# Gated mix of two state-space convolutions: a Tanh gate, a dummy sine, one batch's one-input steps on VectorE, and a new order of the first fifth

## The chip, the cores and the metric

One core of a Trainium2 chip. TensorE (PE in the profile) multiplies matrices into PSUM, VectorE (DVE) and GpSimd (POOL) work element by element, ScalarE (ACT) evaluates functions from a table that it holds and copies, and the SP queue issues most DMAs. The metric is the device time of one execution in microseconds.

## The reference

A gate mixes two S4D convolutions of the same input x of 2048 steps by 512 channels, with 128 modes to a channel:

```python
g = _sigmoid((x * gate_w).sum(-1, keepdims=True))
a = _A_ref(x, A_log_A_real, A_A_imag, A_C_real, A_C_imag, A_log_dt, A_D_skip)
b = _B_ref(x, B_log_A_real, B_A_imag, B_C_real, B_C_imag, B_log_dt, B_D_skip)
return g * a + (1 - g) * b
```

Each of the two computes, with L = 2048:

```python
dt = jnp.exp(log_dt)
A = -jnp.exp(log_A_real) + 1j * A_imag
C = (C_real + 1j * C_imag) * dt[:, None]
P = jnp.exp((A * dt[:, None])[:, :, None] * pos[None, None, :])
K = 2.0 * jnp.einsum("dn,dnl->dl", C, P).real
y = jnp.fft.irfft(Uf * Kf[None, :, :], L2)[:, :, :L]
return y + u * D_skip[None, None, :]
```

## The kernel before, in words

**What is computed where.** The 2 x 512 channels form 8 chunks of 128, worked on in 64 units of 16 channels. A unit makes its convolution kernels from two small grids. TensorE makes the phases (`phase`, L509), exact up to whole turns, by fp16 matmuls of the angles (`rot`, and a constant, `ones`) with a table of times (`cph`). ScalarE takes the magnitude (`magnitude`, L518) and a sine of it as the cosine (`cosine`, L525), and the sine (`sine`, L522). GpSimd multiplies decays into grids (`grid0`, `grid1`, L530) from the bases `bas`, VectorE multiplies sines and cosines into the grids (L551 to L573), TensorE sums over the modes (`modes`, L575). Then come a fast Fourier transform in three matmul steps (`first`, `s2`, then products with the transform of the input on VectorE, `inverse`) and the last step (`final`, `last`), whose matrix `eg` has the gate in it.

**The gate.** `gate` (L778) sums x times gate weights over the channels into all partitions by matmuls; `gate_sig` (L786) takes the sigmoid on ScalarE, with a scale per partition (`sgn`, +1 for kernel a, -1 for b); `gate_e` (L789) multiplies it into a quarter of `eg` on VectorE. There are four quarters, j = 0 to 3; their input is loaded by 16 DMAs `load_ut` (256 KB each).

**The preparation.** Chunks are prepared in five batches: 0; 1 and 2; 3 and 4; 5 and 6; 7. `decay_rate` (L333) takes an Exp of the decay rates on ScalarE. `prep_ops` (L338) makes, in about 35 steps, the angles per step and of the amplitudes: some steps on VectorE or ScalarE by their source or function (`magnitudes`, `larger`, `signs` at L376, `angle` at L384, an Arctan and two Sin), and the others on an engine `E`, VectorE for batch 0 and GpSimd for the later ones. Among those, the one-input steps are `theta` (L380), all that `ts` makes (L392: scaling, rounding to whole turns) and `diag` (L416, a scaled identity). `bounce` spills the angles to DRAM, `turns` (L489) reads them back transposed into `rot`, `turned` (L421) transposes decays and amplitudes by matmuls, `dec` (L429) multiplies them by times, and `make_bases` (L495) takes four Exp a chunk from them into `bas`; `amplitudes` (L500) finishes them on GpSimd.

**Tables on ScalarE.** Before an instruction whose function the table at hand doesn't hold, the compiler puts a table load into ScalarE's queue.

**The order.** The program makes a list of 2494 operations, each of a few instructions, with names such as `al` (`decay_rate`), `ex` (`make_bases`), `gs` (`gate_sig`), `gu` (`load_ut`), `wu` (groups of warm-up matmuls, L286, whose results nobody reads). `ORDER` (L33) is a permutation of that list. It sets the order of every engine's queue, each working through its own in order. `SLOTS` (L191) gives the PSUM bank, of eight, for each PSUM tile in order of allocation.

## Time and profile before

| | |
|---|---|
| runs, us | 501.21, 501.22, 504.62 (median 501.22) |
| profiled execution, us | 500.83 |
| its span, us | 498.9 |
| granted TensorE clock, mean | 0.983 |

Busy time over the span, and instructions:

| engine | busy us | share | instructions |
|---|---|---|---|
| TensorE, matmul | 443.1 | 89% | 12448 |
| TensorE, weight load | 357.4 | 72% | 12448 |
| VectorE | 392.9 | 79% | 864 |
| ScalarE | 405.2 | 81% | 816 |
| GpSimd | 332.9 | 67% | 316 |

The chain that ended last lies 61% on TensorE over the whole span, 12% on ScalarE, 8% on VectorE and 7% on GpSimd. How to read the rows that follow: a row of the timeline or of the chain has start, duration, engine, source line, operation, output and inputs, and in brackets the idle time in front and what ended it. A row of a group has the count, then total busy us and mean ns, then idle time in front. A row by stage has the stretch, its length, and each engine's busy time with its number of instructions. L numbers are lines of the kernel before.

### The profile page before, as it was taken

What the parts mean: (1) busy time and instruction counts of PE and PEld (TensorE: products, weight loads), DVE (VectorE), ACT (ScalarE), POOL (GpSimd) and SP (SyncE); (2) the same over time, 40 slices, a digit from 0 to 9 for tenths busy, and PEclk for the clock granted to TensorE, in tenths of its full rate; (3) what the DMA queues carried; (4) which work ended last, traced back from release to release, by engine and by line L of the source; (5) the groups of instructions that cost most, each with busy time, mean ns of one, the idle gap of its engine ahead of it and who ended that gap; (6) DMA issues with size and microseconds to landing.
All of it is one profiled execution on the core that took longest, in us unless ns stands there. A gap on an engine that the chain in (4) does not pass through costs nothing.

```text
span 498.9 us, 27908 instructions
## 1 busy us (share of the span) xinstructions
PE 443.1 (89%) x12448; PEld 357.4 (72%) x12448; DVE 392.9 (79%) x864; ACT 405.2 (81%) x816; POOL 332.9 (67%) x316
## 2 busy tenths in 40 slices
PE   5967997988999887997999898978998899989988
PEld 5855556876778675875888686767777779767984
DVE  6394898899999975888889795787999898976402
ACT  5697999989899987788998997777999797964323
POOL 1497998899997977686667866385775754862000
PEclk9998999999999999998999998999999999999999
DMA  4669705316550704246430744134443733174201
GB/s 143 226 235 287 186 11 126 69 25 123 136 94 12 150 27 98 69 77 157 79 61 11 150 105 74 57 78 96 113 77 60 157 65 67 36 169 74 59 25 60
DMA packets 32279, 48.92 MB, mean 98 GB/s; under 512 B 10144, under 2 KB 17440, under 8 KB 32160
## 3 DMA queue, kind: packets, MB, share of 16 engines
q1 hardware_dynamic: 27360, 31.41, 22.2%
q0 software_dynamic: 4800, 15.73, 19.0%
q8 instruction: 97, 1.59, 1.3%
q14 instruction: 22, 0.18, 0.1%
HBM read 17.25 MB, written 5.77 MB: 46 GB/s over the span
## 4 chain that ended last, share of the span: by engine, by line
PE 61%; ACT 12%; DVE 8%; issue 8%; POOL 7%; DMA 5%; SPq 0%; DVEq 0%; ACTq 0%; POOLq 0%
PE ps L640 15%; PE psi L694 11%; PE pk L581 9%; PE p0s L514 7%; PE ps L603 5%; DMA xall<-xall 5%; PE pf L718 4%; POOL f L530 3%; PE psu L603 3%; ACT bas L498 2%; ACT xall L610 2%; PE pw L289 2%; PE pw L293 2%; PE psg L782 1%; DVE xall L651 1%
## 5 line engine op out<-in xcount | busy, mean ns | idle before, releaser
L530 POOL TENSOR_TENSOR f<-bas 128x1024 f32<-128x1024 f32 (+1 forms) x128 | 207.7, 1689 | 78.6 <-PE pk L581 45.4
L640 PE MATMUL ps<-xall,gk 128*64 128x64 f32 (+1 forms) x1728 | 111.3, 251 | 5.7 <-DVE f L553 1.7
L640 PEld LDWEIGHTS ps<-xall,gk 128*64 128x64 f32 (+1 forms) x1728 | 101.4, 153 | 19.1 <-issue 2.7
L651 DVE TENSOR_TENSOR xall<-ps,v 128x256 f32<-128x256 f32 x256 | 94.5, 415 | 15.5 <-PE ps L640 13.4
L581 PE MATMUL pk<-f,f 128*32 128x64 f32 x4096 | 74.3, 223 | 15.5 <-issue 7.2
L581 PEld LDWEIGHTS pk<-f,f 128*32 128x32 f32 x4096 | 62.9, 111 | 27.6 <-issue 17.2
L694 PE MATMUL psi<-mi,xall 128*128 128x128 f32 x512 | 71.8, 287 | 4.4 <-issue 2.7
L681 POOL DMA_DIRECT2D xall<-xall x60 | 60.1, 1152 | 17.4 <-DVE f L557 8.1
L694 PEld LDWEIGHTS psi<-mi,xall 128*128 128x128 f32 x512 | 63.5, 196 | 10.2 <-issue 5.0
L557 DVE TENSOR_TENSOR f<-f,p0c 128x512 f32<-128x512 f32 x64 | 43.6, 682 | 14.4 <-ACT p0c L526 13.8
L514 PE MATMUL p1s<-cph,ones 64*128 64x512 f16 x128 | 49.3, 386 | 3.2 <-DVE ks L591 2.1
L553 DVE TENSOR_TENSOR f<-f,p0c 128x512 f32<-128x512 f32 x64 | 43.6, 681 | 8.6 <-ACT p0c L526 7.9
L603 PEld LDWEIGHTS ps<-w,ks 64*64 64x64 f32 x2048 | 35.4, 140 | 20.7 <-issue 7.7
L514 PE MATMUL p0s<-cph,ones 64*128 64x512 f16 x128 | 49.4, 386 | 0.5 <-ACT xall L610 0.4
L514 PE MATMUL p1s<-cph,rot 64*128 64x512 f16 x128 | 49.0, 382 | 0.8 <-issue 0.8
L569 DVE TENSOR_TENSOR f<-f,p1c 128x512 f32<-128x512 f32 x64 | 43.6, 682 | 7.3 <-ACT p1c L526 5.6
L610 ACT COPY xall<-ps 128x512 f32<-128x512 f32 x64 | 36.9, 612 | 15.0 <-PE ps L603 15.0
L603 PE MATMUL ps<-w,ks 64*64 64x64 f32 x2048 | 40.3, 227 | 9.6 <-issue 6.3
L514 PE MATMUL p0s<-cph,rot 64*128 64x512 f16 x128 | 48.9, 382 | 0.0
L701 ACT COPY z<-psi 128x512 f32<-128x512 f32 x64 | 37.9, 609 | 12.7 <-PE psi L694 12.7
L573 DVE TENSOR_TENSOR f<-f,p1s 128x512 f32<-128x512 f32 x64 | 43.6, 681 | 5.2 <-ACT p1s L523 4.1
L565 DVE SCALAR_TENSOR_TENSOR f<-f,p0s 128x512 f32<-128x512 f32 x64 | 43.4, 680 | 3.2 <-ACT p0s L523 3.0
(128 smaller groups left out, 824.1 us busy)
## 6 DMA issues: line engine op xcount, KB each, us to landing
xall<-xall POOLq DMA_DIRECT2D x60, 256.0 KB, 5.2
v<-v SPq DMA_DIRECT2D x64, 128.0 KB, 3.3
uraw<-in_us SPq DMA_DIRECT2D x16, 256.0 KB, 3.8
z<-in_ut SPq DMA_DIRECT2D x16, 256.0 KB, 6.4
out_dram<-ot SPq DMA_DIRECT2D x28, 128.0 KB, 2.2
par<-in_par SPq DMA_DIRECT2D x8, 256.0 KB, 4.4
gk<-in_gk SPq DMA_DIRECT2D x4, 512.0 KB, 6.1
eg<-in_eg SPq DMA_DIRECT2D x4, 512.0 KB, 5.6
```

The source lines that it names most:

```text
L514: PE.matmul(ps, w[h : h + 64], cph[h : h + 64, j], start=j == 0, stop=j == 3, tile_position=(h, 0))
L530: G.tensor_tensor(o.rearrange("p k (a b) -> p k a b", b=8), x[:, :, hi : hi + n].unsqueeze(3).to_broadcast([128, 16, n, 8]), x[:, :, lo : ...
L553: V.tensor_tensor(f0[:, 0, :, 0:32], f0[:, 1, :, 0:32], half(u, p0c[u], True), OP.mult)
L557: V.tensor_tensor(f0[:, 0, :, 32:64], f0[:, 1, :, 32:64], half(u, p0c[u], False), OP.mult)
L569: V.tensor_tensor(f[:, 0], f[:, 1], p1c[u], OP.mult)
L581: PE.matmul(pk[32 * kd : 32 * kd + 32, i, :], f1[:, p, 4 * i + kd, :], f0[:, p, 4 * i + kd, :], start=p == 1, stop=p == 0, tile_position=( ...
L603: PE.matmul(ps[h][64 * ri : 64 * ri + 64, n, :], x[r], w1[r, ri, r], start=True, stop=True, tile_position=(64 * h, 64 * ri),)
L610: S.copy(o, pxs[key][h])
L640: PE.matmul(ps[h : h + w, j, 0:n], gk[:, k, h : h + w], xall[:, x0:x1, 2 * k : 2 * k + 2], start=True, stop=True, tile_position=(0, h),)
L651: V.tensor_tensor(k.rearrange("p x (k t) -> p k x t", t=2), p2s[b, g][:, :, 0:64].rearrange("p k (x t) -> p k x t", t=2), vv.unsqueeze(3). ...
L681: G.dma_start(out=xk(b)[o, s], in_=t2[t, s], accum_op=OP.add)
L694: PE.matmul(ps[:, i, :], t[:, x : x + 2, :].rearrange("p x k -> p (x k)"), w, start=n == 0, stop=n == len(parts) - 1,)
```

## The change

Six things, in code:

- The gate's Sigmoid becomes a Tanh of half the argument (`sgn` is +0.5 and -0.5), and `gate_e` multiplies `eg` by 1 + tanh; the factor 1/2 of sigmoid(x) = (1 + tanh(x/2))/2 goes into the constant `eg`.
- A new operation `tw` takes a Sin of the one-column tile `warm`, which nobody reads. The clearing of `warm` becomes an operation of its own (`fw`).
- In `prep_ops` the one-input steps `theta`, `ts` and `diag` run on an engine `F`, VectorE for batches 0 and 1 and GpSimd for the later ones. The steps with two inputs stay on `E`.
- The list has 2496 operations, and the numbers in `ORDER` are shifted by the two new ones.
- The order is another one up to position 547 of the list (545 before), which is where chunk 2's `turns` stands, next to unit 10's and 11's operations. Behind it the sequence is the one from before.
- `SLOTS` is new. Behind the 115th PSUM tile the banks are those from before, renamed by one permutation.

```diff
@@ fixed @@
-        V.memset(warm, 0.0)
...
     op("fx", fixed)
+    op("fw", V.memset, warm, 0.0)
@@ prep_ops @@
         E = V if i == 0 else G
+
+        F = V if i < 2 else G
...
         def theta():
             for n, c in enumerate(cs):
-                E.tensor_scalar(get("t0")[:, n], pars[i][:, n, 0], dti[:, c : c + 1], None, op0=OP.mult)
+                F.tensor_scalar(get("t0")[:, n], pars[i][:, n, 0], dti[:, c : c + 1], None, op0=OP.mult)
...
         def ts(o, x, s0, s1, op0, op1=None):
             kw = dict(op1=op1) if op1 is not None else {}
-            return lambda: E.tensor_scalar(get(o), get(x), s0, s1, op0=op0, **kw)
+            return lambda: F.tensor_scalar(get(o), get(x), s0, s1, op0=op0, **kw)
...
         def diag():
             d["dg"] = prep.tile([128, 2, 128], F32, name="dg", tag="dg")
             for n, c in enumerate(cs):
-                E.tensor_scalar(d["dg"][:, n], ident, dt2[:, c : c + 1], None, op0=OP.mult)
+                F.tensor_scalar(d["dg"][:, n], ident, dt2[:, c : c + 1], None, op0=OP.mult)
@@ new, behind amplitudes @@
+    def table(f):
+        S.activation(warm, warm, f)
@@ gate_sig, gate_e @@
     def gate_sig(j):
-        S.activation(psg[j], psg[j], AF.Sigmoid, scale=sgn)
+        S.activation(psg[j], psg[j], AF.Tanh, scale=sgn)
...
         g = psg[j].rearrange("p (r m) -> p r m", m=M)
-        V.tensor_tensor(e, e, g.unsqueeze(1).to_broadcast([128, 2, 16, M]), OP.mult)
+        V.scalar_tensor_tensor(e, g.unsqueeze(1).to_broadcast([128, 2, 16, M]), 1.0, e, op0=OP.add, op1=OP.mult)
@@ batch @@
+        if i == 0:
+            op("tw", table, AF.Sin)
         op("al", decay_rate, i)
@@ _layout @@
-    eg = np.stack([np.cos(ph), -np.sin(ph)], 1) / 2048
+    eg = np.stack([np.cos(ph), -np.sin(ph)], 1) / 4096
...
-    small = np.concatenate([ldt, 1 - 2 * kern[:, None], gw, times], 1)
+    small = np.concatenate([ldt, 0.5 - kern[:, None], gw, times], 1)
```

What the new order moves, queue by queue (numbers in parentheses are units, chunks or quarters; a batch's name stands for its step):

- ScalarE, front. Before: magnitudes of batch 0, an input copy, angle, `al`, high parts, low parts, an input copy, the four `ex` of chunk 0, two input copies, magnitude and cosine of unit 0. Now: magnitudes, `al`, an input copy, angle, high parts, low parts, an input copy, the four `ex`, two input copies, `tw`, magnitude and cosine of unit 0.
- ScalarE, gates. Before: `al` of batch 2, the four `ex` of chunk 1, a copy, gates 0 and 1; later gates 3 and 2, parts of batch 1, a copy, the `ex` of chunk 2. Now: `al` of batch 2, a copy, one `ex` of chunk 1, gate 1, the magnitudes of batch 2, `ex`, gate 0, `ex`; later, behind unit 6's last sine, `ex` of chunk 1, gate 2, low parts of batch 1, `ex` of chunk 2, gate 3, a copy, and the other three `ex` of chunk 2.
- TensorE, front. Before four groups of warm-up matmuls stand ahead of batch 0's `turned` and two behind the second input transform; now three stand ahead of `turned`, one between it and the second input transform, two behind that.
- VectorE, front. The clearing of `ones` and `rot` goes behind `dec` of batch 0, the scaled identity of batch 0 ahead of the high parts. Batch 1's scaled identities stand behind that, ahead of unit 0's products; its other one-input steps stand between products of units 1 to 5.
- GpSimd. Batch 1's one-input steps are gone from between the grids of units 0 to 5. From unit 9's large grid to unit 11's small one, its list has batch 2's steps 10 and 16 of `prep_ops` (counted from 0), which stood ahead of that, and no longer its step 8.
- SP queue, front. Ahead of batch 0's `bounce` stand five `load_ut` where three stood; `cph` is issued between `bounce` and `turns` of chunk 0, where it stood ahead of both; `dl` goes behind `gk`. The 16 `load_ut` and four `load_e` are mixed anew up to about the first gates, and `turns` of chunk 2 goes behind the first two turns of `v` of the second block.

## The prediction

> **What bounds the kernel now.** I read the page first, then the busy time by stage, then the chain of waits over the stretch whose order changes, then ScalarE's timeline there.

> ```profile
> span 498.9 us, 27908 instructions
> ```
> ```profile
> core 0: us, PE busy (x) PEld busy (x) DVE busy (x) ACT busy (x) POOL busy (x), PEclk, DMA share, GB/s
> 24.00:42.00 18.00, 10.86 (x349) 8.40 (x348) 15.99 (x31) 16.18 (x34) 17.23 (x18) 1.00 0.76 255
> 42.00:62.00 20.00, 19.03 (x407) 11.89 (x407) 12.63 (x24) 18.50 (x35) 16.28 (x20) 0.91 0.80 222
> 62.00:86.00 24.00, 20.40 (x378) 12.87 (x368) 22.35 (x43) 23.85 (x41) 22.22 (x24) 0.98 0.24 61
> 86.00:106.00 20.00, 19.64 (x429) 17.04 (x430) 18.62 (x39) 18.40 (x39) 18.21 (x18) 0.94 0.32 62
> 106.00:126.00 20.00, 17.06 (x492) 13.02 (x490) 19.44 (x41) 18.17 (x38) 19.51 (x20) 1.00 0.50 102
> ```
> ```profile
> 7.65 8.41 PE pw L289 x64
> ...
> 17.89 3.06 ACT bas L498 x4
> ...
> 38.79 3.11 issue
> ...
> 81.16 1.28 ACT L526
> ...
> 89.54 1.95 POOL f L530
> ```

> The new order ends at about 106 us (unit 10's last sine product on VectorE); behind that every queue holds the same instructions in the same order, and the PSUM banks are only renamed. So the question is how much sooner the engines reach that point. From 106 to 126 us VectorE and GpSimd are busy 19.4 and 19.5 of 20 us, so a shift of all engines there should pass to the end whole, and a lead of GpSimd alone should not.

> In the stretch itself ScalarE is the tightest: 23.85 of 24 us in the third row, 76.9 of 82 in the first four. The chain says the same: it starts on the warm-up matmuls, goes through the four base exponentials, stalls once on the tensor engine (38.79, waiting for nothing that the trace shows), runs on ScalarE around both pairs of gates, table loads such as that at 81.16 among them, and only from 89.54 on lies on GpSimd for long. That GpSimd is busy 17.23 of 18 us early on is for the most part beside it.

> **The front.** The rows of ScalarE's timeline, with start, duration and line:

> ```profile
> 8.29 1.28 ACT L385 ACT_TABLE_LOAD   x1
> 9.59 0.31 ACT L385 ACTIVATE rc<-rc 128x128 f32<-128x128 f32 x1
> 9.92 1.28 ACT L386 ACT_TABLE_LOAD   x1
> ...
> 11.74 1.28 ACT L336 ACT_TABLE_LOAD   x1
> ...
> 14.47 0.52 ACT L409 ACTIVATE sp<-tb 128x384 f16<-128x384 f32 x1 [0.62 <-DVE tb L406]
> ...
> 23.07 0.58 ACT L520 ACTIVATE p0c<-p0s 128x512 f32<-128x512 f32 x1 [1.17 <-PE p0s L514]
> 23.67 1.28 ACT L526 ACT_TABLE_LOAD   x1
> 24.96 0.58 ACT L526 ACTIVATE p0c<-p0c 128x512 f32<-128x512 f32 x1
> ```

> The decay exponential (L336) moves ahead of the angle, to a place where ScalarE waits for the input transform, with or without a load of its own; the arctangent and the sine keep their two loads, since the dummy sine stands behind the exponentials of the bases and not ahead of the arctangent. The exp load thus leaves 11.74 and comes back ahead of the base exponentials. The turned matmuls stand behind three groups of warm-up matmuls and no longer four: 8.41/4 = 2.10 us sooner. On ScalarE the low parts (L409) end at about 14.5, a copy and the load follow, and the exponentials can start at about 16.3, 1.6 before their 17.89. The dummy sine then loads its table in the 1.17 us in which ScalarE waits for the first phase, so that the cosine follows the magnitude at once. The tensor engine still has six warm-up groups, both input transforms and the turned matmuls in front of the first phase, end to end, so that this starts at most 0.35 us sooner than now; the magnitude then starts at about 22.7 and the cosine at 23.3, where it starts at 24.96: **-1.65 us**. GpSimd's first grid gets its bases some 1.6 us sooner too, and the two scaled identities of batch 1 (L419) leave the space between its grids.

> What is moved past what: on the SP queue five gate inputs now go ahead of the first spill of the angles and not three; cph (512 KB, used by the first phase) goes behind that spill. It is issued near 15.2 instead of 9.05, about 6.4 us ahead of the phase. Nearest price:

> ```profile
> cph<-in_cph SPq DMA_DIRECT2D x1, 512.0 KB, 5.8
> ```

> So 0.6 us are left. If cph lands in its old 5.8 us I cost it at nothing; if traffic costs it 2 us more, the front's gain is gone and no more, since the phase is what it holds up.

> **The gates.** Sigmoid (L787) has its own load each time, between one for Exp and one for Sin (the load at 81.16 in the chain is the second pair's):

> ```profile
> 44.20 0.41 ACT L385 ACTIVATE rc<-rc 128x256 f32<-128x256 f32 x1
> ...
> 59.65 1.28 ACT L787 ACT_TABLE_LOAD   x1
> ...
> 72.56 1.28 ACT L787 ACT_TABLE_LOAD   x1
> ```

> In the new order both pairs of gates stand among the exponentials. If Tanh is served by the table that serves Exp, two loads go: 2 x 1.30 (a load and the gaps of 0.01 to 0.02 around it) = **-2.6 us**, both in a stretch where ScalarE is full. The bounds: no table shared, six loads more (a rival below); shared, two fewer. The nearest row is the sine table, under which batch 1's arctangent (L385 at 44.20) starts without a wait and without a load in front of it; tables here hold several functions, so I take sharing. A switch costs what the rows show, 1.28 plus 0.02. [...]

> The new product of the gate is a two-operation instruction instead of a plain one; a pair of such forms of equal size:

> ```profile
> L557 DVE TENSOR_TENSOR f<-f,p0c 128x512 f32<-128x512 f32 x64 | 43.6, 682 | 14.4 <-ACT p0c L526 13.8 <-POOL f L530 0.3
> L565 DVE SCALAR_TENSOR_TENSOR f<-f,p0s 128x512 f32<-128x512 f32 x64 | 43.4, 680 | 3.2 <-ACT p0s L523 3.0
> ```

> 682 against 680 ns: nothing. The halved constants are made on the host.

> **Batch 1's one-input steps.** On GpSimd, grouped over 25 to 62 us by line (L394, L382, L419; busy, count):

> ```profile
> 25.00:62.00 37.00, 7.76 (x8) 0.95 0.78 237
> 25.00:62.00 37.00, 1.18 (x2) 0.95 0.78 237
> 25.00:62.00 37.00, 1.20 (x2) 0.95 0.78 237
> ```
> ```profile
> L394 DVE TENSOR_SCALAR tb<-tb 128x128 f32<-128x128 f32 x4 | 0.9, 222 | 0.0
> ```
> ```profile
> L378 DVE TENSOR_SCALAR sg<-par x5: 286/596/1078, 4.9 to 224.8; 128x512 f32<-128x512 f32 x3, 128x256 f32<-128x256 f32 x2
> ```

> GpSimd loses 10.1 us. I give that no gain of its own: the chain lies on it only from 89.54, and from that grid to unit 11's small grid its new list has one step of batch 2 more than the old one (7.76/8 = 0.97 us at most), for which the 1.8 us that it idles in the fourth row are the cover. VectorE gains twelve instructions, two of them in front, where it waits for the phase. The ten others cost 0.29 us each (the 128x256 minimum), 2.9 us.

> But they may have to wait. The five instructions of L378 are the only one-input SBUF ones that VectorE runs beside grids. The one of 286 ns ran before the grids; the other of that size, at 224.79, took 1078 and ended just after GpSimd's small grid did, so it waited 0.79. By 64 ns more per 128 elements (222 to 286) the 128x512 ones should take about 414 and took 610 on average. That is 0.2 for three, 0.79 for one: 0.35 us on average. Bounds: 0 and a whole grid, 1.95 (the row at 89.54). I take 0.35, so ten cost 6.4 us. Behind each waits the unit's product and then the modes on the tensor engine. What hides them: VectorE idles 2.0 + 7.4 us in the first two rows, of which 1.5 lie ahead of its first product, behind the cosine that ends at 25.54. That leaves some 7.7, so 6.4 fit, barely; the ScalarE gain of the first pair of gates takes another 1.3 of it. VectorE is what is late next. Part of the cover is the stall at 38.79; if it is gone, the ten cost up to 2 us.

> **Sum:** 500.83 us for the profiled run (1.9 outside the span of 498.9) - 1.65 - 2.6 = 496.6. The median of the runs, 501.22, lies 0.4 above the profiled one: forecast **497.0 us**.

> **Rivals.**
> *More comes free.* With loads spread differently the stall at 38.79 goes and ScalarE's wait behind it with it. ScalarE idles 5.1 us in the first four rows; half of that gives 494.4, all of it 491.9. For: ScalarE is short of work there only in that one place. Against: VectorE has no room to follow. Chance 0.25.

> *VectorE becomes the bound.* Each of the ten waits out half a large grid, 0.98 us: 12.7 us, less 7.7 of idle time, is +5.0; the front's and the second pair's gains (-1.65 - 1.3) leave +2.0, so 503.3; with half the idle time unusable +5.9, 507.1. It decides from a mean wait of 0.78 us, or 0.39 if only half the idle time can be used. For: the 1078 ns. Against: three of four waited 0.2. [...] Chance 0.2.

> *Tanh is not in exp's table.* Then the change doesn't save loads: gates and exponentials alternate, six loads around each pair of gates for three now, 6 x 1.30 = +7.8, less 1.65: 507.4. [...] Chance 0.05.

> *The front is late*, cph or the spilled angles holding up the first phase: 498.6 and up to 501. Chance 0.1.

> **Numbers.** Forecast 0.4 (495 to 499). Within 1% of 501.22 (what a measurement of this kernel can tell from no change), 496.2 to 506.2, lie some two thirds of the forecast, the late front, a part of the first rival and most of the second: 0.43. Faster by more: a third of the forecast and most of the first rival, 0.41. Slower by more: the third rival and the second's upper part, with some room for a cost not seen, 0.16. The range runs from the first rival's end, 491.9, to past the second's middle: 491.5 to 504.

> **What would show it.** Right: two table loads fewer, none between base exponentials and gates; the first cosine at 23.3; the sine load behind the second pair of gates, now 81.16, near 77; unit 10's last product on VectorE some 4 us sooner; from there the same distance to the end. Wrong: VectorE's L394 of 128x256 at a mean over 1.0 us, and VectorE full from 42 to 62 us; a first phase that starts after 21.95; a lead at 106 us that shrinks later.

## The result, and the profile after

| | before | after |
|---|---|---|
| executions, us | 501.21, 501.22, 502.39, 504.62 | 505.52, 506.03, 509.24, 509.49 |
| median, us | 501.81 | 507.63 |
| ratio, 95% interval | | 1.0101 [1.0059, 1.0143] |
| profiled execution, us (clock) | 500.83 (0.983) | 506.03 (0.99) |

The kernel became 1% slower; 497.0 was forecast. Ten more executions of after, in a later run, gave 505.57 against 502.75 (1.0069 [1.0032, 1.0106]). Executions of one and the same kernel lie up to 16 us apart in these runs. So every ratio has its interval; it is taken over undisturbed executions alone, the medians over all, and the two can differ.

The head of after's page, and its busy time by stage in the stretches shown of before:

```profile
span 503.5 us, 27931 instructions
```
```profile
core 0: us, PE busy (x) PEld busy (x) DVE busy (x) ACT busy (x) POOL busy (x), PEclk, DMA share, GB/s
24.00:42.00 18.00, 12.12 (x416) 10.04 (x420) 16.51 (x32) 16.07 (x35) 9.27 (x9) 1.00 0.67 227
42.00:62.00 20.00, 18.70 (x394) 11.08 (x384) 18.95 (x35) 19.57 (x39) 14.86 (x15) 1.00 0.80 235
62.00:86.00 24.00, 21.52 (x442) 14.33 (x444) 23.45 (x47) 23.85 (x44) 23.61 (x26) 1.00 0.43 99
86.00:106.00 20.00, 17.58 (x349) 15.32 (x338) 16.57 (x36) 16.13 (x34) 19.07 (x20) 0.91 0.12 23
106.00:126.00 20.00, 16.22 (x488) 12.82 (x488) 19.93 (x36) 18.51 (x39) 19.33 (x18) 1.00 0.55 112
```

GpSimd's 17.23 us of the first stretch are 9.27, and VectorE's 12.63 of the second are 18.95: VectorE gained 6.8 us in the first two stretches, where 6.4 were forecast. ScalarE still idles 1.9 us in the first stretch, where it idled 1.8 (the two loads that went lay behind it). The order did what it says. ScalarE's timeline:

```profile
17.02 3.05 ACT L500 ACTIVATE bas<-dec 128x896 f32<-128x896 f32 x4
...
22.33 0.20 ACT L509 ACTIVATE warm<-warm 128x1 f32<-128x1 f32 x1
23.56 0.58 ACT L526 ACTIVATE p0c<-p0s 128x512 f32<-128x512 f32 x1 [1.03 <-PE p1s L520]
24.18 0.58 ACT L532 ACTIVATE p0c<-p0c 128x512 f32<-128x512 f32 x1
...
77.25 1.28 ACT L532 ACT_TABLE_LOAD   x1
```

The first cosine (L532) starts at 24.18, before at 24.96. The sine load behind the second gates is at 77.25, before at 81.16, and there is no load between base exponentials and gates: the gate at 71.34 (L793) follows an exponential at 70.42 (L500) without one, and after has 23 table loads in all for 25 in before. Tanh does sit in exp's table. At unit 12, behind the part that was reordered, this is the magnitude on ScalarE in after and in before:

```profile
111.45 0.62 ACT L526 ACTIVATE p0c<-p0s 128x512 f32<-128x512 f32 x1
```
```profile
113.68 0.62 ACT L520 ACTIVATE p0c<-p0s 128x512 f32<-128x512 f32 x1
```

So this pair of executions has a lead of 2.2 us there, in place of 4.2, and in the unchanged rest it turns into a loss of 4.6. One execution each shows little of a lead of that size: in the profiles below, the same start lies between 110.39 and 113.85 us in before's order (117.09 with 96 fewer) and between 110.05 and 113.85 in after's with Tanh.

**Where the rest lost it.** These are pieces of before's chain of waits past 120 us, the longest of those in which an engine waits for nothing that the profile names (start and duration in us):

```profile
175.27 2.45 issue
193.89 2.83 issue
233.85 1.18 issue
300.37 2.26 issue
342.84 1.51 issue
438.49 1.70 issue
491.45 1.38 issue
```

and of after:

```profile
125.67 2.88 issue
175.15 2.37 issue
193.35 3.24 issue
213.12 1.19 issue
234.64 1.21 issue
290.52 1.49 issue
302.80 2.28 issue
316.61 1.57 issue
343.72 2.31 issue
446.15 2.11 issue
464.42 1.13 issue
488.42 1.68 issue
```

Past 170 us these are seven pieces with 13.3 us in before and eleven with 20.6 in after, in the same work in the same order. Number all rows of the tensor engine in the trace (weight loads, matmuls, semaphore events) from 0, and divide the number by 256: the remainder (mod) is the same for all of these stalls in after past 170 us. Some of them:

```
after: number  mod 256  resumes at  idle  end of the last 16 KB instruction packet
        7105     193      177.52    2.37    176.00
        8129     193      196.58    3.23    195.13
        9153     193      214.31    1.19    212.89
       13249     193      292.01    1.49    290.44
       14017     193      305.08    2.28    303.66
```

All 17 stalls over 0.5 us in after that wait for no semaphore stand at position 193 of 256, and the engine goes on 1.20 to 1.56 us after a packet of this queue, a row of after's profile page, has landed:

```profile
q8 instruction: 97, 1.59, 1.3%
```

Two kinds can be told apart. In the first, the page is short. Half of after's packets start 0.9 to 1.7 us after the page in front of them has been entered (median 1.1); a packet takes about 1 us, and the engine can go on some 1.45 us later. By these medians, a page that is passed in under some 3.6 us should end in a stall (an estimate), and that hangs on which 256 instructions make up the page. In after, of the pages with no late packet, 12 of the 17 passed in less than that ended in a stall of over 0.1 us, and 4 of the 65 others. In the second, the packet is late; counted here as late is one that starts 2.4 us or more after that (the latest, 7.0). At 175 and 194 us in after it starts 4.2 to 4.5 us after, about when the engine stops or later. So it is (4.9 us) at 38.79 in before, the stall of 3.11 that the prediction could not name, which stands at position 193 too. Late packets make up 14.1 of after's 28.1 us of stalls at position 193, and 13.3 of before's 23.9. What makes a packet late isn't shown.

After has the same 12,448 matmuls, and 17 semaphore events more on the tensor engine than before (181 for 164), all of them in the reordered part. So the whole unchanged rest sits 17 places further on in its pages. That is the first theory (**pages**). It has two rivals. One is the renamed PSUM **banks**. The other is VectorE held up by GpSimd (**lock**), for which this row of after speaks, beside its like in before:

```profile
122.62 3.34 DVE L380 TENSOR_SCALAR sg<-par 128x512 f32<-128x512 f32 x1
```
```profile
124.69 0.50 DVE L378 TENSOR_SCALAR sg<-par 128x512 f32<-128x512 f32 x1
```

The sign step of batch 3, unchanged, took 2.8 us longer, the tensor engine stood still for 2.8 beside it, and the whole lead of 2 us was gone at unit 15.

### The profile page after: what moved, and what is told of

It reads as the page before. It is cut to its first block, busy times and chain, and to the rows that moved or that the text cites. A ratio compares the mean times of both kernels' runs of the same rounds, so it can differ in the third digit from the quotient of the medians.

```text
span 503.5 us, 27931 instructions
## 1 busy us (share of the span) xinstructions
PE 439.7 (87%) x12448; PEld 355.6 (71%) x12448; DVE 401.0 (80%) x876; ACT 404.0 (80%) x815; POOL 322.9 (64%) x304
## 3 DMA queue, kind: packets, MB, share of 16 engines
q0 software_dynamic: 4800, 15.73, 18.9%
## 4 chain that ended last, share of the span: by engine, by line
PE 52%; ACT 13%; issue 10%; POOL 9%; DVE 9%; DMA 6%; SPq 1%; DVEq 0%; ACTq 0%
PE ps L646 14%; PE psi L700 11%; PE pk L587 8%; PE p0s L520 6%; POOL f L536 5%; PE ps L609 4%; PE pf L724 4%; DMA v<-v 2%; ACT xall L616 2%; PE psu L609 2%; PE pw L292 2%; DVE xall L657 1%; DMA gk<-in_gk 1%; DVE f L579 1%; ACT p1c L526 1%
## 5 line engine op out<-in xcount | busy, mean ns | idle before, releaser
L563 DVE TENSOR_TENSOR f<-f,p0c 128x512 f32<-128x512 f32 x64 | 43.6, 681 | 12.8 <-ACT p0c L532 10.5
L559 DVE TENSOR_TENSOR f<-f,p0c 128x512 f32<-128x512 f32 x64 | 43.6, 682 | 10.1 <-ACT p0c L532 10.1
L520 PE MATMUL p0s<-cph,rot 64*128 64x512 f16 x128 | 48.2, 376 | 3.2 <-issue 3.2
L520 PE MATMUL p1s<-cph,ones 64*128 64x512 f16 x128 | 48.6, 380 | 2.1 <-DVE f L563 1.2
L609 PEld LDWEIGHTS ps<-w,ks 64*64 64x64 f32 x2048 | 34.9, 137 | 20.6 <-issue 8.0
L520 PE MATMUL p0s<-cph,ones 64*128 64x512 f16 x128 | 48.8, 381 | 0.5 <-DVE f L563 0.4
L520 PE MATMUL p1s<-cph,rot 64*128 64x512 f16 x128 | 48.1, 376 | 0.2 <-issue 0.2
L571 DVE SCALAR_TENSOR_TENSOR f<-f,p0s 128x512 f32<-128x512 f32 x64 | 43.4, 679 | 2.3 <-ACT p0s L529 2.0
## 6 DMA issues: line engine op xcount, KB each, us to landing
gk<-in_gk SPq DMA_DIRECT2D x4, 512.0 KB, 7.8
eg<-in_eg SPq DMA_DIRECT2D x4, 512.0 KB, 6.9
```

The costliest lines, as they stand in the source:

```text
L520: PE.matmul(ps, w[h : h + 64], cph[h : h + 64, j], start=j == 0, stop=j == 3, tile_position=(h, 0))
L559: V.tensor_tensor(f0[:, 0, :, 0:32], f0[:, 1, :, 0:32], half(u, p0c[u], True), OP.mult)
L563: V.tensor_tensor(f0[:, 0, :, 32:64], f0[:, 1, :, 32:64], half(u, p0c[u], False), OP.mult)
L609: PE.matmul(ps[h][64 * ri : 64 * ri + 64, n, :], x[r], w1[r, ri, r], start=True, stop=True, tile_position=(64 * h, 64 * ri),)
```

## The experiments

Each time stands against executions of before taken beside it. "Fewer" and "more" count tensor instructions in front of everything else, and the place is that count, with 17 added for after. The columns that the warm-up multiplies stay the same, and nobody reads its results.

**Moving the pages.** The forecast of the theory was worked out from the traces: take the start of each numbered instruction, leave the stalls at 193 out, cut the list into pages of 256, and sum what each page past 70 us lacks of 3.6 us; a shift moves the cuts. This sum is the forecast lack.

```diff
 def warm_up(n):
     pw = bank("pw")
-    for i in range(8):
-        PE.matmul(pw[:, 0:128], ident, ident, start=True, stop=True)
+    for w in WIDTHS.get(n, [128] * 8):
+        x = ident[:, 0:w] if w <= 128 else ident.unsqueeze(1).to_broadcast([128, w // 128, 128])
+        PE.matmul(pw[:, 0:w], ident, x, start=True, stop=True)
```

After, `WIDTHS = {2: [512, 256, 128, 128]}`:

> After, with the last warm-up group on the tensor engine cut to four matmul calls that cover the same 1024 columns (512, 256, 128, 128 instead of eight of 128): the same tensor time within 0.1 us, but 16 instructions fewer ahead of everything else, so that the rest of the tensor engine's list falls on nearly the same 256-instruction pages as in before. Nothing of the output hangs on it. Page theory (the lost time of the second half is the tensor engine waiting for its own instructions at position 193 of a page, and the change lost it by 17 more instructions in front): summed over the pages of after's trace, the shortfall against 3.6 us a page goes from 14.6 to 10.7 us, so the time falls by 2.5 to 4.5 us, to 503 to 505; VectorE's long sign step of batch 3 near 123 us may stay. Lock theory (VectorE held up by GpSimd is the whole loss): no change, 505.5 to 509.5. Bank theory (the renamed PSUM banks): no change.

Before, `{1: [128] * 4 + [64] * 8}`:

> Before, with its last warm-up group made of twelve matmul calls for the same 1024 columns (four of 128, eight of 64): 16 instructions more in front, nothing else touched, and nothing of the output hangs on it. Page theory: the shortfall against 3.6 us a page goes from 10.0 to 18.9 us, of which the stall at 38.79 (3.1 us) goes and the later ones grow, so 3 to 8 us slower than before, 505 to 510, with the new stalls all at position 193 of a page and new ones near 213 and 290 us as in after. Lock theory and bank theory: no change, 501 to 503, or 3 us faster by the stall at 38.79.

After as it is:

> After once more, unchanged, on the chip of the runs beside it, so that they have a base of their own. All theories: 1.0% over before, 503 to 510 by the granted clock. The sign step of batch 3 near 123 us: the lock theory, if the long step is a matter of the moment at which it is issued, gives either 0.5 us or more than 3 us; if it belongs to after's order, more than 3 us again.

After, `{2: [512, 512], 5: [512, 512]}`:

> After, with its last two warm-up groups made of two matmul calls of 512 columns each: 48 instructions fewer in front, the same columns. The page theory has a number for every shift: summed over the pages of six traces, the shortfall against 3.6 us a page is 14.6 us for after, 10 for 16 fewer, and has its least value, 4.6, at 48 fewer. A sixteenth-step of 4 us was worth 3.4 us between the two runs of the first call, so 10 us should be worth 6 to 8.5: 499 to 502 by the granted clock, 2 to 4 us faster than before. The stalls at position 193 past 170 us should sum to under 12 us, where after has 24 to 28. Lock and bank theories: as after.

Before, `{1: [512, 512], 2: [256, 256, 128, 128, 128, 128]}`:

> Before, with its last two warm-up groups made of two calls of 512 columns, and of two of 256 and four of 128: 32 instructions fewer, the same columns. Page theory: the shortfall past 70 us goes from 10.0 to 3.5 us, and the 3.1 us at 38.79 go, so 4 to 6 us faster than before, 496 to 500, with no more of after's parts in it. Lock and bank theories: 0, or 3 us at most by the stall at 38.79.

Before, `[512, 512]` for groups 0, 1, 2 and 4:

> Before, with four of its six warm-up groups made of two calls of 512 columns: 96 instructions fewer, the same columns. It parts the page theory from its nearest rival, that fewer and larger warm-up calls are themselves what made the kernel faster with 32 fewer. Page theory: the shortfall past 70 us goes from 10.0 (before) and 3.5 (32 fewer) up to 21.5 us, so 4 to 9 us slower than before, 506 to 511. Rival: as fast as with 32 fewer or faster, 495 or below.

The pair at 48 and 32 fewer, once more:

> After with 48 instructions fewer, once more, for the size of the difference at equal pages. If the change's gain is there but was hidden by few runs: 2 us or more under before with 32 fewer, 493 to 495 where that has 496 to 497. If the gain is gone: the same within 1 us, or 1 to 2 us above.

> Before with 32 instructions fewer, once more: 495 to 498, 1 to 1.6% faster than before, and the other half of the pair at equal pages.

| kernel | place against before | forecast lack, us | median, us | before, us | ratio, 95% |
|---|---|---|---|---|---|
| before, 96 fewer | -96 | 21.5 | 507.71 | 502.57 | 1.0096 [1.0046, 1.0146] |
| before, 32 fewer | -32 | 3.5 | 495.69 | 502.75 | 0.9841 [0.9766, 0.9916] |
| the same again | -32 | 3.5 | 498.10 | 503.46 | 0.9806 [0.9744, 0.9867] |
| after, 48 fewer | -31 | 4.6 | 500.24 | 502.75 | 0.9926 [0.9878, 0.9974] |
| the same again | -31 | 4.6 | 499.98 | 503.46 | 0.9886 [0.9835, 0.9937] |
| before | 0 | 10.0 | | | 1 |
| after, 16 fewer | +1 | 10.7 | 504.29 | 503.90 | 1.0054 [1.0002, 1.0107] |
| before, 16 more | +16 | 18.9 | 506.39 | 503.90 | 1.0067 [1.0016, 1.0119] |
| after | +17 | 14.6 | 505.57 | 502.75 | 1.0069 [1.0032, 1.0106] |

The pages hold in sign, and but for +16 and +17, which are level, in order, for both kernels and in both directions. 32 fewer make before 1.6 to 1.9% faster and 96 fewer make it 1% slower, so it isn't that fewer or larger warm-up matmuls are better. 16 more take before, with its own banks and its own order, to where after is: banks and lock are not needed for that. Nor is it the granted clock: with the clock's line taken off (last section), before with 32 fewer is still 5.1 and 4.0 us faster, with 96 fewer 3.6 us slower and with 16 more 3.2 us slower.

The traces put the difference where the theory has it, in the unchanged rest. From unit 12's magnitude to the end it takes 385.9 us on average in the ten profiles at -32 and -31 (379.8 to 391.0), 388.2 in the three at 0 and +1, 391.5 in the six at +16 and +17 (387.7 to 395.1), and 393.1 in the one at -96. Single profiles scatter by more than that.

Two things came out otherwise than forecast. The size is between a quarter (16 more) and the whole (32 fewer) of the difference in the list. And the stalls at 193 past 110 us don't sum to under 12 us at the best place: they are 19.2 and 24.9 in before with 32 fewer, for 21.0 in before and 26.6 in after. Over the whole kernel they come to 23.2 us on average at -32 and -31, 26.7 from 0 to +17 and 31.9 at -96. That is the right order, but less of a difference than in the times, and the remainder isn't explained. Late packets occur in both kernels, 12 in before and 15 in after.

With that the rows at equal places can be read for the change itself. By the medians it costs 0.4 us at 0 and +1, 4.6 and 1.9 at -32 and -31, and is about level at +16 and +17; by the ratios it costs 0.5% at 0 and +1 and 0.8 to 0.9% at -32 and -31, where the intervals overlap. The change's own gain of 4.2 us isn't there at all. In after itself, going from +17 to +1 is worth 2.4 us by the medians and 0.8 by the ratios, with intervals that overlap. So the 17 places are a part of after's loss, not the whole of it.

**The gates.** Tanh alone, in before, and in before with 32 fewer:

```diff
-        S.activation(psg[j], psg[j], AF.Sigmoid, scale=sgn)
+        S.activation(psg[j], psg[j], AF.Tanh, scale=sgn)
```

> Before with Tanh for Sigmoid alone (halved constants, the two-operation product of the gate), in before's order and with the same tensor list: two table loads fewer, near 59.65 and 72.56. The gate step of the prediction, alone: ScalarE 2.6 us ahead behind the second gates, and 499.2 if that reaches the end whole. Page theory: the pages don't move, so the stalls past 170 us are those of before within 2 us in sum, and the gain comes through to 1.5 us or more (498.5 to 500.5). If the tail eats a lead whatever the pages are: 501 to 502.

> Before with 32 instructions fewer, as before, and Tanh for Sigmoid on top: the gate step of the prediction where the pages cost least. If the pages were what ate the 2.6 us of the two loads, 2 us or more faster than with 32 fewer alone, 493 to 494. If ScalarE's lead ends on work of the tensor engine at 86 to 100 us whatever the pages are: within 1 us of 32 fewer alone, 495 to 496.5.

And Sigmoid put back, in after with 48 fewer, where its place among the exponentials should cost eight loads more (8 x 1.30 us, an estimate from the loads above):

> After with 48 instructions fewer and Sigmoid in the place of Tanh (with its constants and plain product), in after's order: eight table loads more, 8 x 1.30 = 10.4 us more on ScalarE between 56 and 76 us. If what ScalarE gains or loses there reaches the end whole, as the prediction's gate step has it: 10 us slower than with 48 fewer alone, 508 to 511. If other engines hold the place where ScalarE's lead ends (unit 9 to 12) and have some 2 us to spare: 6 to 8 us slower. If ScalarE isn't the bound there at all: under 3.

Tanh in before: 502.58 against 503.90, 0.9984 [0.9934, 1.0034]. With 32 fewer: 494.84, where 32 fewer alone had 495.69 and 498.10 (0.9872 [0.9777, 0.9967], where 32 fewer alone had 0.9841 and 0.9806). Both are 1 to 3 us better by the medians, the second is worse by the ratios, and neither shows a gain of Tanh that can be told from none. Sigmoid in after's order: 510.18 against 499.98 beside it, 10.2 us for the 10.4 estimated. But its executions also had a lower granted clock (0.963 to 0.976 for 0.976 to 0.99); with the clock's line taken off, 5.7 us are left, and in its trace unit 12 comes 5.2 and 8.2 us later than in the two of after with 48 fewer. So at least half of a delay of ScalarE there reaches the end; that it does so whole isn't shown. A lead doesn't show. What may eat it in after comes below; for before with Tanh alone it stays open (its profiled execution had a sign step of 3.31 us too, and a stall of 4.01 at the page end near 42 us).

**The sign step of batch 3.**

```diff
-            V.tensor_scalar(both("sg"), c, 0.0, 0.5, op0=OP.is_ge, op1=OP.subtract)
+            V.tensor_scalar(both("sg"), c, 0.0, 0.5, op0=OP.is_ge, op1=OP.subtract, accum_out=junk)
```

for batch 3 alone, the form that also writes its accumulator, which nobody reads: in after, in after with 48 fewer, in before with 32 fewer.

> [...] Lock theory: the step falls from 3.34 to about 0.7 us, unit 14's cosine products end some 2.5 us sooner, the tensor engine's idle 2.8 us at 124.5 shrinks below 1, and the total falls by 2 to 2.9 us, to about 505. Page theory: the 2 us at unit 15 come back as well, but the loss from unit 25 on (4 us) stays, since the pages are the same; if the lead gets eaten there, the total falls by less than 1 us.

> After with 48 instructions fewer and batch 3's sign step in the form that writes its accumulator, which took 0.68 us beside GpSimd in the first call where the plain form took 0.5 to 3.34. Lock theory: in those executions in which the plain form waits (3.3 us in two of ten profiles, 0.9 in two) unit 15 comes sooner, so the mean falls by 0.5 to 1 us against 48 fewer alone, and the highest times by 2 or more. Otherwise: no change within the noise of 1 us.

> Before with 32 instructions fewer and batch 3's sign step in the form that writes its accumulator (0.68 us whatever GpSimd does). Lock theory: the mean falls by 0.3 to 1 us against 32 fewer alone, since the plain form waits for 0.4 to 2.9 us in a part of the executions. Otherwise the same, or 0.2 slower by the longer form.

VectorE's row of the first of these:

```profile
L382 DVE TENSOR_SCALAR_CACHE_REDUCE sg<-par x1: 679/679/679, 124.8 to 124.8; 128x512 f32<-128x512 f32 x1
```

It took 0.679 us there and 0.678 in after with 48 fewer; that it takes this whatever GpSimd does isn't shown by two profiles. The plain form took 0.49 to 0.52 us in seven profiles, 0.93 to 0.95 in seven, and 3.3 in two, one of after and one of before's order with Tanh: it is a matter of the moment and belongs to neither kernel. The 3.34 us reach over the ends of three GpSimd instructions and close 0.3 us behind the third. The times: after 509.54 (1.0164 [1.008, 1.0247], four executions, no faster than after), with 48 fewer 497.45 (0.9883 [0.9818, 0.9948]) against 500, before with 32 fewer 499.30 (0.9799 [0.9699, 0.9899]) against 498.10. One better, one worse, one the same: that the long step costs 2 us in an execution that has it is seen in the trace; that the form pays on the mean isn't shown.

**The moved steps.** All back on GpSimd, then the angle step alone, in after with 48 fewer:

```diff
-        F = V if i < 2 else G
+        F = V if i < 1 else G
```

> After, with batch 1's one-input steps back on GpSimd, in after's order: the move alone undone, the tensor engine's list and its pages the same. The prediction's step (the ten steps lie in VectorE's idle time, GpSimd's relief worth nothing): within 1 us of after. VectorE as the bound: 2 to 3 us faster than after by the waits of 2.9 us and the 2.9 us of the steps. GpSimd as the bound: 2 to 4 us slower than after, unit 10 later by as much, since GpSimd gets 10.1 us back.

```diff
-                F.tensor_scalar(get("t0")[:, n], pars[i][:, n, 0], dti[:, c : c + 1], None, op0=OP.mult)
+                E.tensor_scalar(get("t0")[:, n], pars[i][:, n, 0], dti[:, c : c + 1], None, op0=OP.mult)
```

> After with 48 instructions fewer and batch 1's angle step alone (the two products with the step width, line 384 of after) back on GpSimd; the other steps stay on VectorE. If its wait for GpSimd's grids eats the gain: no VectorE instruction of 2 to 3 us near 31 us, ScalarE's idle 2.3 and 1.0 us near 36 us gone, unit 12 some 2 to 3 us sooner than with 48 fewer alone, and the total 2 to 3 us lower, 497 to 498 where that has 500. If the wait lies beside other work: the same within 1 us. If GpSimd's 1.2 us for the step hold up its next grid: 1 us slower.

> The same with batch 3's sign step in the form that writes its accumulator as well, which was 2.6 us faster on the mean of ten executions than 48 fewer alone. If both waits for GpSimd count and add up: 4 to 5 us under 48 fewer alone, 495 to 496, 1.5% faster than before and 2.3% than after. If only the first: 497 to 498.

All back: 505.50, after 505.57 beside it, but 1.0023 [0.9983, 1.0062] for 1.0069 by the ratios: from nothing to 2 us better, not settled. The traces show a wait that came with the move. After with 16 fewer, GpSimd's, VectorE's, the tensor engine's and ScalarE's timelines:

```profile
30.59 2.99 POOL L537 TENSOR_TENSOR f<-bas 128x1024 f32<-128x1024 f32 x2 [3.07 <-PE pk L588]
...
30.68 2.97 DVE L385 TENSOR_SCALAR tb<-par,dti 128x128 f32<-128x128 f32 x2
33.58 0.68 DVE L564 TENSOR_TENSOR f<-f,p0c 128x512 f32<-128x512 f32 x1
...
34.35 1.97 PE L647 MATMUL ps<-xall,gk 128*64 128x64 f32 x32 [2.55 <-ACT al L337]
...
36.36 0.93 ACT L669 COPY v<-ps 128x256 f32<-128x256 f32 x3 [2.40 <-PE ps L647]
37.96 1.07 ACT L617 COPY xall<-psu 128x512 f32<-128x512 f32 x2 [0.68 <-PE psu L610]
```

A product of the angle step (L385) of this size took 0.28 us for batch 0, ahead of all grids, in after and in before. Here the two begin 0.09 us behind two grids that GpSimd runs back to back, and each ends 0.08 us behind one of these grids (1.95 and 1.10 us). Behind them stands a cosine product (L564); 0.1 us after its end the tensor engine goes on, having stood for 2.55 us. (The profile puts that wait down to an exponential on ScalarE, which ended 0.4 us earlier; in after and in after with 48 fewer the tensor engine also goes on 0.1 us after L564.) ScalarE, which copies its results, idles 2.40 and 0.68 us. That is more than the 2.6 us of the two table loads. In seven of nine profiles with this step on VectorE it took 2.2 to 3.0 us (2.24 in the profile of after); in the other two it took under 0.6, and the tensor engine has no such wait there. With the step on GpSimd, in after with 48 fewer:

```profile
30.22 0.68 DVE L560 TENSOR_TENSOR f<-f,p0c 128x512 f32<-128x512 f32 x1
30.82 0.68 DVE L564 TENSOR_TENSOR f<-f,p0c 128x512 f32<-128x512 f32 x1
...
30.55 2.58 PE L647 MATMUL ps<-xall,gk 128*64 128x64 f32 x64
...
33.40 0.69 ACT L337 ACTIVATE al<-par,small 128x128 f32<-128x128 f32 x2
33.99 0.90 ACT L669 COPY v<-ps 128x256 f32<-128x256 f32 x3
34.78 1.09 ACT L617 COPY xall<-psu 128x512 f32<-128x512 f32 x2
```

There is no wait on any of the three. ScalarE is busy 17.88 of the 18 us from 24 to 42 (16.53 with the sign step changed as well), with the step on VectorE 14.83 in the profile above and 14.64 and 14.59 in those with 48 fewer. How much of that arrives behind the reordered part isn't settled: unit 12's magnitude starts at 110.05 and 112.63 in the two profiles with the step on GpSimd, and at 110.86 and 113.85 in the two of after with 48 fewer.

| after, 48 fewer | sign step plain | with accumulator |
|---|---|---|
| angle step on VectorE | 500.24, 499.98 | 497.45 |
| angle step on GpSimd | 495.54 | 497.60 |

495.54 against 503.20 is 0.979 [0.9739, 0.984] of before, so it beats both kernels; before with 32 fewer does so as well and as much. With both edits it is 0.9897 [0.9857, 0.9938], and the gain of the angle step isn't seen there. So the wait, and that it is gone when the step is gone, are shown in the traces; its price in the mean is somewhere between nothing and 4.7 us.

**The front.** The two gate inputs that after issues behind the first block's input, moved behind the second's (operations 96 and 94 behind 80 in `ORDER`):

```diff
-    ... 52, 53, 96, 46, 2, ... 61, 94, 62, ... 72, 80, 71, ...
+    ... 52, 53, 46, 2, ... 61, 62, ... 72, 80, 96, 94, 71, ...
```

> After, with two gate inputs that its order issues right behind the first block's input (and ahead of the first phase's table) moved behind the second block's input; nothing else. Front step of the prediction: it gave 1.65 us and was 0.8 by the profile, with the first input landing 0.9 later than in before. If the two loads beside it are the cause, the first input transform starts at 5.7 again, where after has 6.3 to 6.7, and the first cosine near 23.3. Otherwise it stays at 6.3 or later. On the total: 0.5 to 1 us faster, under what the runs can tell.

The first input transform started at 6.00 us (before 5.67, after 6.53), the first cosine at 24.3: a good half of the delay of the first input went, and nothing of it came through to the cosine. 504.65 against 502.57, 1.013 [1.0073, 1.0187]: no gain. What holds the front up there is open.

## Why the prediction was wrong, by its steps

- **"So a shift of all engines there should pass to the end whole"** (there: from 106 to 126 us): this step failed. It took the same work in the same order to take the same time. The tensor engine's pages aren't part of that order, and 17 semaphore events in the reordered part moved them: worth 2.5 us in before (+16 against 0), and 0.8 to 2.4 in after (+17 against +1, not clear of the noise). In the profiled execution the rest took 392.0 us for 385.2, 2.8 of them in the sign step.
- **The moved steps, "so 6.4 fit, barely"** (into 7.7 us of VectorE's idle time): this step failed too. The mean wait was right (0.29 us over ten instructions in after, 0.35 forecast; L394, feared at a mean over 1.0 us, took 0.43) and the reading of it wrong. It isn't spread: in after, 1.8 of 2.9 us of waiting fall to the first pair, where the tensor engine, and by it ScalarE, wait next. (Nor were the sign steps VectorE's only one-input instructions beside grids: the reciprocal, L453, is another, and it took 1.74 us for 128x256 each time.) "Behind each waits the unit's product and then the modes on the tensor engine" named the place; the sum then set a mean against idle time that lay elsewhere. ScalarE loses some 3 us by it near 36 us. That this is what ate the whole gain isn't shown: the times above allow anything from nothing to 4.7 us for it. At equal places the forecast 4.2 us are missing, and the rest of that stays open.
- **The front, -1.65:** -0.78 in the profile of after. Exponentials at 17.02 for 16.3 forecast, magnitude at 23.56 for 22.7, because the first input landed 0.9 us later (two gate inputs beside it, in part) and the first phase came 0.5 later, at 22.44, not 0.35 sooner; "a first phase that starts after 21.95" was one of the signs of being wrong. The profiles scatter by more: the first cosine starts at 23.38 to 25.56 us in after's order and at 24.31 to 26.32 in before's. Of cph, which it feared for, nothing was seen.
- **The gates, -2.6:** the loads went, Tanh was in exp's table, 77.25 for "near 77". That ScalarE's time counts there is borne out by the 5.7 to 10.2 us that Sigmoid costs in after's order; that a lead of 2.6 counts whole isn't: Tanh alone shows no gain clear of the noise in either place.
- **GpSimd's relief worth nothing:** this holds; with all its steps given back the time was the same or lower.
- **The rivals:** "VectorE becomes the bound" through its wait for GpSimd was the nearest, 503.3 to 507.1 for 507.6, and right that VectorE's steps end where GpSimd's do, though VectorE isn't quite full: 16.5 of 18 us and 18.95 of 20. Each product of the angle step ended 0.08 us behind one grid; but the sign step, a single instruction, reached over the ends of three GpSimd instructions (3.34 us), and in the form with an accumulator it took 0.68. Why VectorE waits there isn't shown. "More comes free" took the stall at 38.79 for a matter of loads; there the instruction packet was late, landing at 40.44, and the engine went on 1.46 us behind it. Tanh was in exp's table, and the front was late, but not by cph or the spilled angles.
- **"A lead at 106 us that shrinks later"** stood among the things that would prove it wrong, and the profiled pair shows it.

## What to carry to other kernels

Where a chain shows "issue" on an engine with tens of thousands of small instructions, number the instructions: if the stalls fall on one position modulo the instruction packet, as all 17 over 0.5 us did in after (193 of 256), the code's place in its pages is a parameter like any other, and four wide warm-up matmuls for sixteen narrow ones made after 1.4 to 1.8% faster. Any edit in front that changes the number of instructions shifts it, by 17 places here, so compare edits at equal places, or the place can decide the verdict. And price a VectorE step beside GpSimd's work by the whole run of GpSimd instructions next to it (3.34 us over the ends of three here), at the one place where an engine waits behind it, not by its mean.

## What the runs showed of the hardware

- In after, 12 of 17 pages of 256 tensor instructions passed in under 3.6 us ended in a stall of over 0.1 us, up to 2.3, their packets not being late; at all 17 stalls over 0.5 us the packet landed and 1.20 to 1.56 us later the engine went on. Where the packet starts late, it cost more: 3.24 us at 193 us in after, 2.83 in before.
- One VectorE instruction reached over the ends of three GpSimd instructions in a row: the sign step of batch 3, 3.34 us in after. It took 3.31 in before with Tanh; a sign step of the same size near 37 us took 0.41 to 0.42 in eleven profiles of after's order and 0.73 in before.
- Over the executions of all the experiments, a straight line with a level of its own for each kernel gives some 4 us for each 0.01 of the mean granted clock (0.963 to 0.997), as much as most edits here. What sets the clock isn't shown.
